# The norm's sum of squares as two fp32r products, with pools reordered, sums in place, and a weight load in pieces

## The chip, the cores and the metric

One core of one Trainium2 chip. The metric is the device time of one execution in microseconds. The engines: PE multiplies matrices into PSUM (eight banks of 128 x 512 fp32), DVE, ACT and POOL work on SBUF tiles (DVE and ACT on PSUM too), and SP issues all DMAs, in order.

## The reference, cut to what matters

Chunked attention over q, k, v (4 x 8 x 768 x 64) with 8 memory keys, then two feed-forward layers over 3072 tokens of 512 features:

```python
x = attention(q, k, v, mem_k, mem_v)            # 3072 x 512
h = x @ w_in                                    # 512 -> 2048
g = h * np.tanh(softplus(h))
x = g @ w_out                                   # 2048 -> 512
rms = np.sqrt(np.mean(x * x, axis=-1, keepdims=True) + 1e-06)
xn = x / rms * rms_g
g = xn @ w_gate                                 # 512 -> 1536
out = (g / (1 + np.exp(-g)) * (xn @ w_val)) @ w_out2   # 1536 -> 512
```

## The kernel before

**Numbers in two parts.** A factor is split by `split` (lines 144 to 146) into a high part, cast to fp32r by ACT, and a low part, the difference, by DVE (POOL for some weights). A product is then three matmuls: high by high, high by low, low by high. One product, of the norm, is left in plain fp32.

**Seven products for eight.** `group` (lines 616 to 642) computes a 2 x 2 block product from seven block products of sums, in the order 1, 6, 5, 4, 2, 7, 3, in four banks X, Y, Z, V; ACT and DVE take intermediate sums out of the banks, POOL adds one result. The weights' sums are made once by conversion jobs (`cv_all`; `finish`, line 268, for those w_in weights that were first kept unsummed), the activations' by `sum_pieces` (line 563): four subtractions and seven splits into tiles T.

**Stages.** (1) Attention, mixed with the first layer's first half for the token blocks that are ready: `unit` (plain products) for the first two blocks, then `group1` for the pairs. Results g go to a scratch in HBM. (2) `out1` (line 773): for each of six blocks m of 512 tokens, eight steps i; `Feed` loads g, applies Mish on ACT, splits it and PE multiplies it with w_out into four banks. A step is 24 matmuls. When a block is done, `rms_pieces` (line 784) makes the norm: squares on ACT, three additions on POOL, a product of ones with the sum, which adds over partitions (`p1`, line 800), then the root and the scaling on ACT and DVE. Its pieces are issued one by one between the next block's steps; every second block the T sums of a pair follow and are stored (`nt_scratch`). The last norm runs during the first groups of the next stage. (3) `group2`: twelve weights for each of three pairs; the result s goes to `h_scratch`. (4) `group3` (line 844): twelve units of 128 x 2 x 2 tokens against w_out2; the T tiles of a unit are made by `h_pieces` (line 841) between the seven products of the group before (`preparing`, line 1143). `h_load` (line 823) loads the unit's four blocks b11, b21, b12, b22, for odd units into weight slot 2. The last weight, ("o2", 5), is loaded into slot 3 (line 1176) when group2 of weight 10 no longer needs it.

**Memory.** `cp`, `gp`, `tp` hold group1's temporaries, its results g and the T tiles; they lie in this order on the left of SBUF and are closed after the last group1. The late pools take the same memory from its start: `gl` (4 KB a partition), `c` (2 x 2 KB) and `t` (8 x 8 KB). With `reuse_waits="tile"` a late tile waits for those earlier tiles that lay at its place. `gl` and `gr` hold one tile each for group2's v; `v_temp` (line 555) takes the same two for the temporaries of `sum_pieces`. `sm` (in `cvp`) is one tile of 4 KB.

**What sets the order.** The program is written as pieces issued between products (`between` functions with fixed slots). Then a planner (`schedule_with_timeline_sim`, line 19) orders each engine's instructions by a clock of its own: what is ready by that clock may go ahead of what stands before it. `pin` (`keep_in_program_order`) sets an instruction behind the one that stood before it in the program on its engine. On each engine, and on SP, the queue then runs in that order; an instruction that waits holds all behind it. A tile of a pool is given out in the planner's order too.

Of the kernel before, what the change touches and what calls it, by code (L numbers as in the profile page):

```python
# [29 lines left out]
def tile_kernel(  # L30
# [15 lines left out]
    nc = tc.nc  # L46
# [36 lines left out]
    rawp = ctx.enter_context(tc.tile_pool(name="rawp", bufs=2))  # L83
    cap = ctx.enter_context(tc.tile_pool(name="cap", bufs=3))
    mid_stack = ExitStack()
    cp = mid_stack.enter_context(tc.tile_pool(name="cp", bufs=6))
    gp = mid_stack.enter_context(tc.tile_pool(name="gp", bufs=5))
    tp = mid_stack.enter_context(tc.tile_pool(name="tp", bufs=8))
    late_pools = {}
    psp = ctx.enter_context(tc.tile_pool(name="psp", bufs=1, space=bass.MemoryType.PSUM))  # L90
    bk = [psp.tile([128, 512], F32, name=f"bk{c}") for c in range(6)]
# [3 lines left out]

    ident = const.tile([128, 128], F32, name="ident")
    ones = const.tile([128, 1], F32, name="ones")
    rmsg = const.tile([128, KC], F32, name="rmsg")


# [18 lines left out]
    def as7(s):  # L119
        return s.rearrange("p (a l f) -> p a l f", a=7, l=2)  # L120

    def w_load(key, u):
        s = w_slot(u)
        nc.sync.dma_start(out=s.bitcast(F32), in_=wd[key].bitcast(F32))
        wtab[key] = as7(s)

    def w_store(key, half):
# [140 lines left out]
    def finish(key):  # L268
        w = wtab[key]
        aa = [cap.tile([128, 512], F32, tag="ca", name="ca") for n in range(2)]  # L270
        for n, a in enumerate(aa):
            hi, lo = (w[:, 2 * n:2 * n + 2, l, :].bitcast(F32) for l in range(2))
            nc.vector.tensor_tensor(a.rearrange("p (a f) -> p a f", a=2), hi, lo, op=ALU.add)
        a0, a1 = aa
        a11, a12, a21, a22 = a0[:, 0:256], a0[:, 256:512], a1[:, 0:256], a1[:, 256:512]
        sm = cvp.tile([128, 4, 256], F32, tag="sm", name="sm")
        s4, s1, s2, s3 = (sm[:, i, :] for i in range(4))
        nc.gpsimd.tensor_tensor(s1, a21, a22, op=ALU.add)
        nc.gpsimd.tensor_tensor(s3, a11, a21, op=ALU.subtract)
# [278 lines left out]
    def t_pieces(j, x0, x1, new, temp_new, dram, tab):  # L558

        return sum_pieces(j, x0[:, 0:2, :], x0[:, 2:4, :], x1[:, 0:2, :], x1[:, 2:4, :],  # L560
                          new, temp_new, dram, tab)

    def sum_pieces(j, b11, b21, b12, b22, new, temp_new, dram, tab):
        cols = b11.shape[2]
        size = b11.shape[1] * cols
        temp = {}

        def as_block(x):
            return x[:, 0:size].rearrange("p (a n) -> p a n", n=cols)

        def one(p, src):
            t = new()
            if isinstance(t, tuple):
                split(src, *t)
                for l in range(2):
                    store_later(dram[:, p - 1, l].bitcast(F32), t[l].bitcast(F32))
                return
            v = t.rearrange("p l a n -> p l (a n)")[:, :, 0:size]
            v = v.rearrange("p l (a n) -> p l a n", n=cols)
            split(src, v[:, 0], v[:, 1])  # L580
            if dram is not None:
                store_later(dram[:, p - 1].bitcast(F32), t.bitcast(F32))
            tab[j, p] = v

        def sums():
            for p in (2, 4):
                temp[p] = as_block(temp_new(p).rearrange("p a n -> p (a n)"))
            nc.vector.tensor_tensor(b11, b12, b11, op=ALU.subtract)
            nc.vector.tensor_tensor(temp[2], b22, b11, op=ALU.subtract)
            nc.vector.tensor_tensor(temp[4], temp[2], b21, op=ALU.subtract)  # L590
            nc.vector.tensor_tensor(b12, b22, b12, op=ALU.subtract)

        early = [lambda: one(1, b11), sums]
        rest = [lambda: one(6, temp[2]), lambda: one(5, b11), lambda: one(4, temp[4]),
                lambda: one(2, b21), lambda: one(7, b12), lambda: one(3, b22)]
        return early, rest

# [18 lines left out]
    def group(mul, banks, n_, c12, c21, c22, temps):  # L616

        X, Y, Z, V = banks
        x, y, z, vv = (b_[:, 0:n_] for b_ in banks)
        s1, u2, z5 = temps()  # L620
        mul(1, X, True)
        nc.scalar.copy(s1, x)  # L622
        yield
        mul(6, Y, True)
        nc.vector.tensor_tensor(u2, y, s1, op=ALU.add)
        yield
        mul(5, Z, True)
        nc.scalar.copy(z5, z)
        yield
        mul(4, V, True)  # L630
        yield
        mul(2, X, False)
        yield
        mul(7, Y, False)
        u3 = s1
        nc.vector.tensor_tensor(u3, y, s1, op=ALU.add)  # L636
        yield
        mul(3, Z, False)
        nc.vector.tensor_tensor(c12, z, u2, op=ALU.add)
        nc.gpsimd.tensor_tensor(c22, u3, z5, op=ALU.add)  # L640
# [140 lines left out]

    xn = {}

    def rms_pieces(m, n, new, sq_new):
        xs = new().bitcast(F32).rearrange("p a b n -> p (a b) n")
        xn[n] = xs
        ps = banks1(m)
# [10 lines left out]
                nc.vector.tensor_copy(xs[:, c, :], ps[c])  # L798

        def p1():  # L800
            nc.tensor.matmul(ps[3], ones.to_broadcast([128, 128]), sq[0])
            nc.vector.tensor_scalar(mm, ps[3], 1.0 / DM, EPS_RMS, op0=ALU.mult, op1=ALU.add)

        def p2():
# [34 lines left out]
        hraw[n] = parts  # L839

    def h_pieces(n):
        return sum_pieces(n, *hraw.pop(n), t_new2, v_temp, None, ttab_h)

    def group3(n, j, r, between):
        o = s_new()
# [15 lines left out]
        run([group(mul, banks, 256, c12, c21, c22, lambda: (c_new()[:, 0:256], c12, c22))], between)  # L861
        nc.scalar.copy(o[0][:, 0:256], c11)
        for a in range(2):
            row = (2 * j + a) * N2 + 128 * r
# [5 lines left out]
    for x in vw:  # L870
        nc.gpsimd.memset(x, 0.0)
        nc.gpsimd.memset(x[:, :, :, D:D + 1], 1.0)
    nc.gpsimd.memset(ones, 1.0)

    CV_START = 24
    W_SLOT = (0, 4, 3, 2, 1, 0, 4, 3)
# [171 lines left out]
    late_pools["gl"] = late_pool("gl", 1)  # L1048
    late_pools["c"] = late_pool("c", 2)
    late_pools["t"] = late_pool("t", 8)  # L1050
    pend = []
    sq_new = lambda: [c_new() for _ in range(2)]
    for s, (m, i) in enumerate(steps):
        t = feed.next(s)
        out1(m, i, t)
        flush()
        if i == F1 // 2 - 1 and m < NB2 - 1:
            assert not pend
            p0, pend = rms_pieces(m, m, t_new2, sq_new)
            p0()  # L1060
            if m % 2:
                def both(m=m):
# [29 lines left out]
    def last_temp(p):  # L1092
# [5 lines left out]
    p0, pend = rms_pieces(  # L1098
        NB2 - 1, NB2 - 1,
        lambda: hold[:, 0:4 * N2].rearrange("p (a b n) -> p a b n", a=2, b=2),  # L1100
        lambda: [upper[:, a] for a in range(2)],
    )
    p0()

# [55 lines left out]
    for jn, j in enumerate(jback):  # L1160
# [7 lines left out]
        for f in range(HG + 2 if jn else HG, F2):  # L1168
            run([group2(j, f)], preparing(0, bt) if last and f == F2 - 1 else bt)
            if last and f == HG + 2:  # L1170
                w_load(("o2", 3), 5)
            elif last and f == HG + 3:
                h_load(0, *units[0])
                w_load(("o2", 4), 6)
            elif last and f == HG + 4:
                w_load(("o2", 5), 3)
    h_load(1, *units[1])
    for n, (j, r) in enumerate(units):
        if 0 < n < len(units) - 1:
# [34 lines left out]
```

## Time and profile before

| | us |
|---|---|
| median of 3 runs | 1191.08 (1189.69 to 1196.43) |
| the profiled execution | 1190.69 |
| its span in the trace | 1188.9 |
| PE busy | 1153.8 |
| DVE busy | 817.5 |
| ACT busy | 621.5 |
| POOL busy | 215.1 |

A row of the timeline has the start, the length, the engine, the line, the operation, output and inputs with their shapes, and in brackets how long the engine stood idle before it and what it waited for. Successive matmuls overlap: the distance of starts, not the length, is what one takes of PE's time. PEclk is the granted clock of TensorE as a share of 2.4 GHz; a value between 0.5 and 1 is a mean over the two levels.

### The profile page before, as it was taken

What the parts mean: (1) busy time and instruction counts of PE and PEld (TensorE: products, weight loads), DVE (VectorE), ACT (ScalarE), POOL (GpSimd) and SP (SyncE); (2) the same over time, 40 slices, a digit from 0 to 9 for tenths busy, and PEclk for the clock granted to TensorE, in tenths of its full rate; (3) what the DMA queues carried; (4) which work ended last, traced back from release to release, by engine and by line L of the source; (5) the groups of instructions that cost most, each with busy time, mean ns of one, the idle gap of its engine ahead of it and who ended that gap; (6) DMA issues with size and microseconds to landing.
All of it is one profiled execution on the core that took longest, in us unless ns stands there. A gap on an engine that the chain in (4) does not pass through costs nothing.

```text
span 1188.9 us, 22951 instructions
## 1 busy us (share of the span) xinstructions
PE 1153.8 (97%) x9052; PEld 1008.5 (85%) x9052; DVE 817.5 (69%) x1212; ACT 621.5 (52%) x996; POOL 215.1 (18%) x185
## 2 busy tenths in 40 slices
PE   6899899999999899999999999999999999999998
PEld 4789899999999688888878878878888888999998
DVE  4655898854755856675775675976886746887773
ACT  5566566543545866667665443553454423444442
POOL 2010222310132411030131121322221211000000
PEclk8899989999999999999999999999999999999999
DMA  9889869899488764595589388899889878654420
GB/s 188 172 230 217 209 239 264 231 293 300 148 304 289 246 204 129 187 362 163 195 329 393 144 343 333 321 416 391 319 312 377 315 264 293 195 173 142 142 90 36
DMA packets 219132, 294.20 MB, mean 247 GB/s; under 512 B 104208, under 2 KB 168720, under 8 KB 210064
## 3 DMA queue, kind: packets, MB, share of 16 engines
q1 hardware_dynamic: 219024, 292.73, 74.1%
q8 instruction: 71, 1.16, 0.4%
q14 instruction: 37, 0.30, 0.1%
HBM read 181.80 MB, written 110.89 MB: 246 GB/s over the span
## 4 chain that ended last, share of the span: by engine, by line
PE 74%; DMA 8%; DVE 7%; ACT 5%; issue 3%; POOL 2%; SPq 0%; ACTq 0%; POOLq 0%; DVEq 0%
PE bk L612 13%; PE bk L614 12%; PE bk L613 12%; DMA s<-g_scratch 4%; PE bk L856 4%; PE bk L854 4%; PE bk L855 4%; PE bk L726 3%; PE bk L727 3%; PE bk L725 3%; PE bkp L612 2%; PE bkp L614 2%; PE bkp L613 2%; PE bkp L434 2%; PE bkp L483 1%
## 5 line engine op out<-in xcount | busy, mean ns | idle before, releaser
L612 PE MATMUL bk<-T,w 128*128 128x384 f32 (+1 forms) x860 | 317.3, 372 | 5.5 <-ACT g L662 4.1
L613 PE MATMUL bk<-T,w 128*128 128x384 f32 (+1 forms) x860 | 312.5, 363 | 0.0
L614 PE MATMUL bk<-T,w 128*128 128x384 f32 (+1 forms) x860 | 311.6, 364 | 0.0
L612 PEld LDWEIGHTS bk<-T,w 128*128 128x128 f32 x860 | 162.7, 190 | 26.7 <-ACT g L662 4.3
L613 PEld LDWEIGHTS bk<-T,w 128*128 128x128 f32 x860 | 162.5, 189 | 17.3 <-issue 0.2
L614 PEld LDWEIGHTS bk<-T,w 128*128 128x128 f32 x860 | 162.3, 189 | 16.8
L854 PE MATMUL bk<-w,T 128*128 128x256 f32 x396 | 112.3, 284 | 2.9 <-ACT T L145 1.8
L725 PE MATMUL bk<-T,w 128*128 128x512 f32 x276 | 109.1, 396 | 2.9 <-ACT T L145 2.9
L856 PE MATMUL bk<-w,T 128*128 128x256 f32 x396 | 111.4, 282 | 0.2 <-DVE T L146 0.2
L855 PE MATMUL bk<-w,T 128*128 128x256 f32 x396 | 111.4, 281 | 0.0
L726 PE MATMUL bk<-T,w 128*128 128x512 f32 x276 | 109.4, 396 | 0.3 <-DVE T L146 0.3
L727 PE MATMUL bk<-T,w 128*128 128x512 f32 x276 | 108.6, 393 | 0.0
L640 POOL TENSOR_TENSOR v<-c,v 128x512 f32<-128x512 f32 x36 | 51.6, 1436 | 222.3 <-DVE c L636 164.8
L636 DVE TENSOR_TENSOR c<-bk,c 128x512 f32<-128x512 f32 (+2 forms) x72 | 43.1, 599 | 63.4 <-PE bk L614 51.7
L622 ACT COPY c<-bk 128x512 f32<-128x512 f32 (+2 forms) x72 | 37.0, 516 | 83.9 <-PE bk L614 33.3
L146 DVE TENSOR_TENSOR T<-s,T 128x1024 fp32r<-128x1024 f32 (+1 forms) x50 | 61.3, 1235 | 26.0 <-ACT T L145 25.5
L854 PEld LDWEIGHTS bk<-w,T 128*128 128x128 f32 x396 | 75.2, 190 | 4.2 <-ACT T L145 2.9
L855 PEld LDWEIGHTS bk<-w,T 128*128 128x128 f32 x396 | 75.5, 191 | 0.1
L856 PEld LDWEIGHTS bk<-w,T 128*128 128x128 f32 x396 | 75.0, 190 | 0.4 <-DVE T L146 0.4
L753 ACT ACTIVATE s<-s 128x1024 f32<-128x1024 f32 x44 | 46.7, 1061 | 38.6 <-DMA s<-g_scratch 36.6
L725 PEld LDWEIGHTS bk<-T,w 128*128 128x128 f32 x276 | 51.8, 188 | 15.4 <-ACT T L145 3.3
L726 PEld LDWEIGHTS bk<-T,w 128*128 128x128 f32 x276 | 52.0, 188 | 13.2 <-issue 1.2
(218 smaller groups left out, 2309.2 us busy)
## 6 DMA issues: line engine op xcount, KB each, us to landing
T<-nt_scratch SPq DMA_DIRECT2D x35, 1024.0 KB
g_scratch<-g SPq DMA_DIRECT2D x64, 384.0 KB
s<-g_scratch SPq DMA_DIRECT2D x46, 512.0 KB
h_scratch<-s SPq DMA_DIRECT2D x36, 512.0 KB
w<-wg SPq DMA_DIRECT2D x10, 1792.0 KB
wg<-w SPq DMA_DIRECT2D x30, 512.0 KB
raw<-in_moe_w_out_dram SPq DMA_DIRECT2D x28, 512.0 KB
nt_scratch<-T SPq DMA_DIRECT2D x14, 1024.0 KB
```

The costliest lines, as they stand in the source:

```text
L146: keep((eng or nc.vector).tensor_tensor(lo, src, hi.bitcast(F32), op=ALU.subtract))
L612: nc.tensor.matmul(ps, whi, xh, start=first and kk == 0, stop=False, **more)
L613: nc.tensor.matmul(ps, whi, xl, start=False, stop=False, **more)
L614: nc.tensor.matmul(ps, wlo, xh, start=False, stop=kk == 1, **more)
L640: nc.gpsimd.tensor_tensor(c22, u3, z5, op=ALU.add)
L725: nc.tensor.matmul(ps, ahi, bhi, start=start, stop=False)
L726: nc.tensor.matmul(ps, ahi, blo, start=False, stop=False)
L727: nc.tensor.matmul(ps, alo, bhi, start=False, stop=stop)
L753: nc.scalar.activation(x, g, self.act)
L854: nc.tensor.matmul(ps, t[:, 0, f], w[:, 0], start=first and f == 0, stop=False, **more)
L855: nc.tensor.matmul(ps, t[:, 0, f], w[:, 1], start=False, stop=False, **more)
L856: nc.tensor.matmul(ps, t[:, 1, f], w[:, 0], start=False, stop=f == HG - 1, **more)
```

## The change

Six edits. (a) The pools are opened in the order tp, gp, cp, and Feed's fourth split is called right after the late pools are opened. (b) `p1` splits the sum of squares into a high and a low part (tiles gl and gr in turn, for the last block the tile sm) and multiplies both with ones in fp32r, into the same bank; `ones_r` is a cast copy of ones. The norms advance the counter that alternates gl and gr in group2. (c) `finish` pins its two first additions for the w_in weights 6 and 5. (d) `h_pieces` no longer uses `sum_pieces`: the sums are made in place in b11 and b12, with no temporaries, in the order T1, 5, 6, 2, 4, 7, 3. (e) group3's product 5 comes before 6. (f) The load of ("o2", 5) is three DMAs: the factor of product 1 (256 KB), those of 2, 4 and 3, and those of 5, 6 and 7 (768 KB each). `sum_one` is the former inner function `one`, unchanged.

```diff
@@ pools
+    tp = mid_stack.enter_context(tc.tile_pool(name="tp", bufs=8))
+    gp = mid_stack.enter_context(tc.tile_pool(name="gp", bufs=5))
     cp = mid_stack.enter_context(tc.tile_pool(name="cp", bufs=6))
-    gp = mid_stack.enter_context(tc.tile_pool(name="gp", bufs=5))
-    tp = mid_stack.enter_context(tc.tile_pool(name="tp", bufs=8))
...
+    ones_r = const.tile([128, 1], F32R, name="ones_r")
...
-    def w_load(key, u):
+    def w_load(key, u, cuts=()):
         s = w_slot(u)
-        nc.sync.dma_start(out=s.bitcast(F32), in_=wd[key].bitcast(F32))
+        edges = (0,) + cuts + (7,)
+        for a, b in zip(edges, edges[1:]):
+            at = slice(512 * a, 512 * b)
+            nc.sync.dma_start(out=s[:, at].bitcast(F32), in_=wd[key][:, at].bitcast(F32))
...
@@ finish
-            nc.vector.tensor_tensor(a.rearrange("p (a f) -> p a f", a=2), hi, lo, op=ALU.add)
+            ins = nc.vector.tensor_tensor(a.rearrange("p (a f) -> p a f", a=2), hi, lo, op=ALU.add)
+            if key[1] in (6, 5):
+                pin(ins)
...
@@ group
-        mul(6, Y, True)
-        nc.vector.tensor_tensor(u2, y, s1, op=ALU.add)
-        yield
-        mul(5, Z, True)
-        nc.scalar.copy(z5, z)
-        yield
+        for p in (5, 6) if five_first else (6, 5):
+            if p == 6:
+                mul(6, Y, True)
+                nc.vector.tensor_tensor(u2, y, s1, op=ALU.add)
+            else:
+                mul(5, Z, True)
+                nc.scalar.copy(z5, z)
+            yield
...
@@ rms_pieces
         def p1():
-            nc.tensor.matmul(ps[3], ones.to_broadcast([128, 128]), sq[0])
+            parts = parts_new()
+            split(sq[0], parts[0], parts[1])
+            for l in range(2):
+                nc.tensor.matmul(
+                    ps[3], ones_r.to_broadcast([128, 128]), parts[l], start=l == 0, stop=l == 1
+                )
             nc.vector.tensor_scalar(mm, ps[3], 1.0 / DM, EPS_RMS, op0=ALU.mult, op1=ALU.add)
...
     def h_pieces(n):
-        return sum_pieces(n, *hraw.pop(n), t_new2, v_temp, None, ttab_h)
+        b11, b21, b12, b22 = hraw.pop(n)
+        one = lambda p, src: sum_one(n, p, src, t_new2, None, ttab_h)
+        sub = lambda out, a, b: nc.vector.tensor_tensor(out, a, b, op=ALU.subtract)
+        early = [lambda: one(1, b11), lambda: sub(b11, b12, b11), lambda: sub(b12, b22, b12)]
+
+        def p5():
+            one(5, b11)
+            sub(b11, b22, b11)
+
+        def p6():
+            one(6, b11)
+            sub(b11, b11, b21)
+
+        return early, [p5, p6, lambda: one(2, b21), lambda: one(4, b11),
+                       lambda: one(7, b12), lambda: one(3, b22)]
...
+    nc.scalar.copy(ones_r, ones)
...
     late_pools["t"] = late_pool("t", 8)
+    feed.split(4)
...
+    def v_parts():
+        n_v[0] += 1
+        x = v_new(n_v[0]).bitcast(F32R)
+        return [x[:, l, :] for l in range(2)]
...
-                w_load(("o2", 5), 3)
+                w_load(("o2", 5), 3, (1, 4))
```

## Rows read from the trace of the kernel before

**Rows 1.** The page, part 1: busy time, share of the span, instructions.

```profile
PE 1153.8 (97%) x9052; PEld 1008.5 (85%) x9052; DVE 817.5 (69%) x1212; ACT 621.5 (52%) x996; POOL 215.1 (18%) x185
```

**Rows 2.** Busy time by stretch: length, engines, PEclk, DMA share, GB/s.

```profile
145.00:150.00 5.00, 1.23 (x4) 1.23 (x5) 5.00 (x7) 2.49 (x5) 1.66 (x2) 0.81 1.07 310
...
150.00:155.00 5.00, 5.00 (x70) 4.02 (x68) 5.00 (x9) 5.00 (x10) 0.00 (x0) 0.51 0.89 353
...
396.00:400.00 4.00, 3.71 (x10) 2.61 (x10) 3.97 (x6) 4.00 (x6) 0.00 (x0) 0.66 0.21 59
...
1040.00:1160.00 120.00, 120.00 (x1008) 120.00 (x1007) 96.14 (x123) 53.73 (x81) 8.73 (x8) 1.00 0.45 137
```

**Rows 3.** Timeline of PE, 392 to 401 us: start, length.

```profile
392.53 0.40 PE L727 MATMUL bkp<-w 128*128 128x512 f32 x1
...
395.80 0.73 PE L725 MATMUL bk<-T,w 128*128 128x512 f32 x2 [2.87 <-ACT T L145]
...
400.81 0.40 PE L725 MATMUL bk<-T,w 128*128 128x512 f32 x1
```

**Rows 4.** Timeline of ACT, 387 to 396 us.

```profile
387.74 1.06 ACT L753 ACTIVATE sm<-w 128x1024 f32<-128x1024 f32 x1 [0.19 <-DVE w L146]
...
394.70 1.05 ACT L145 CAST T<-sm 128x1024 fp32r<-128x1024 f32 x1 [0.94 <-DMA g_scratch<-g]
```

**Rows 5.** Timeline of PE around the first product with ones.

```profile
436.27 0.40 PE L727 MATMUL bk<-T,w 128*128 128x512 f32 x1
...
437.59 0.39 PE L726 MATMUL bk<-T,w 128*128 128x512 f32 x1
...
437.82 0.40 PE L727 MATMUL bk<-T,w 128*128 128x512 f32 x1
```

**Rows 6.** Timeline of PE at the fifth norm, then groups by form.

```profile
616.85 1.12 PE L801 MATMUL bkp<-c,ones 128*128 128x512 f32 x2 [0.42 <-POOL c L796]
...
L753 ACT ACTIVATE s<-s 128x1024 f32<-128x1024 f32 x44 | 46.7, 1061 | 38.6 <-DMA s<-g_scratch 36.6 <-DVE T L146 1.8
L146 DVE TENSOR_TENSOR w<-ca,w 128x512 fp32r<-128x512 f32 x31 | 23.7, 764 | 9.7 <-ACT w L145 9.6
L145 ACT CAST w<-ca 128x512 fp32r<-128x512 f32 x47 | 29.1, 618 | 17.1 <-DVE ca L208 14.7 <-DMA wg<-w 2.2
```

**Rows 7.** Timeline of DVE, then of PE, 140 to 149 us.

```profile
140.00 0.69 DVE L273 TENSOR_TENSOR ca<-w 128x512 f32<-128x512 f32 x1
...
141.40 1.28 DVE L273 TENSOR_TENSOR ca<-w 128x512 f32<-128x512 f32 x2
...
144.46 0.94 DVE L588 TENSOR_TENSOR xb<-xb 128x768 f32<-128x768 f32 x1
...
145.99 1.49 DVE L589 TENSOR_TENSOR g<-xb 128x768 f32<-128x768 f32 x1
...
148.77 0.69 PE L612 MATMUL bk<-T,w 128*128 128x384 f32 x1 [4.07 <-ACT g L662]
```

**Rows 8.** 1000 to 1030 us: stretches as in rows 2, timelines, chain of waits.

```profile
1000.00:1005.00 5.00, 3.46 (x22) 2.73 (x21) 4.61 (x6) 3.85 (x6) 0.00 (x0) 1.00 0.70 291
1020.00:1025.00 5.00, 3.56 (x23) 2.95 (x24) 5.00 (x8) 4.29 (x6) 0.00 (x0) 1.00 0.29 108
1025.00:1030.00 5.00, 5.00 (x44) 5.00 (x43) 4.97 (x7) 0.78 (x3) 0.00 (x0) 1.00 0.28 83
...
1001.74 0.95 DVE L590 TENSOR_TENSOR v<-v,raw 128x768 f32<-128x768 f32 x1
...
1003.13 0.39 PE L854 MATMUL bk<-w,T 128*128 128x256 f32 x1 [0.97 <-DMA w<-wo]
...
1005.93 0.59 ACT L628 COPY v<-bk 128x512 f32<-128x512 f32 x1
...
996.13 6.96 DMA w<-wo
...
1010.77 4.23 DMA w<-h_scratch
```

More of the change, by code (lines that the diff above doesn't have):

```diff
@@ L561, in t_pieces, with sum_one @@
                           new, temp_new, dram, tab)
+    def sum_one(j, p, src, new, dram, tab):
+        cols = src.shape[2]
+        size = src.shape[1] * cols
+        t = new()
+        if isinstance(t, tuple):
+            split(src, *t)
+            for l in range(2):
+                store_later(dram[:, p - 1, l].bitcast(F32), t[l].bitcast(F32))
+            return
+        v = t.rearrange("p l a n -> p l (a n)")[:, :, 0:size]
+        v = v.rearrange("p l (a n) -> p l a n", n=cols)
+        split(src, v[:, 0], v[:, 1])
+        if dram is not None:
+            store_later(dram[:, p - 1].bitcast(F32), t.bitcast(F32))
+        tab[j, p] = v
     def sum_pieces(j, b11, b21, b12, b22, new, temp_new, dram, tab):
@@ L569, in as_block @@
             return x[:, 0:size].rearrange("p (a n) -> p a n", n=cols)
[L571 to L583, printed above, removed]
+        one = lambda p, src: sum_one(j, p, src, new, dram, tab)
         def sums():
@@ L614, in product, with group @@
             nc.tensor.matmul(ps, wlo, xh, start=False, stop=kk == 1, **more)
-    def group(mul, banks, n_, c12, c21, c22, temps):
+    def group(mul, banks, n_, c12, c21, c22, temps, five_first=False):
         X, Y, Z, V = banks
@@ L782, in tile_kernel, with rms_pieces @@
     xn = {}
-    def rms_pieces(m, n, new, sq_new):
+    def rms_pieces(m, n, new, sq_new, parts_new):
         xs = new().bitcast(F32).rearrange("p a b n -> p (a b) n")
@@ L800, in p1 @@
         def p1():
-            nc.tensor.matmul(ps[3], ones.to_broadcast([128, 128]), sq[0])
+            parts = parts_new()
+            split(sq[0], parts[0], parts[1])
+            for l in range(2):
+                nc.tensor.matmul(
+                    ps[3], ones_r.to_broadcast([128, 128]), parts[l], start=l == 0, stop=l == 1
+                )
             nc.vector.tensor_scalar(mm, ps[3], 1.0 / DM, EPS_RMS, op0=ALU.mult, op1=ALU.add)
@@ L860, in group3 @@
         c12, c21, c22 = o[1][:, 0:256], o[0][:, 256:512], o[1][:, 256:512]
-        run([group(mul, banks, 256, c12, c21, c22, lambda: (c_new()[:, 0:256], c12, c22))], between)
+        run([group(mul, banks, 256, c12, c21, c22, lambda: (c_new()[:, 0:256], c12, c22),
+                   True)], between)
         nc.scalar.copy(o[0][:, 0:256], c11)
@@ L1050, in tile_kernel, with sm_parts @@
     late_pools["t"] = late_pool("t", 8)
+    feed.split(4)
     pend = []
     sq_new = lambda: [c_new() for _ in range(2)]
+    def v_parts():
+        n_v[0] += 1
+        x = v_new(n_v[0]).bitcast(F32R)
+        return [x[:, l, :] for l in range(2)]
+    def sm_parts():
+        x = cvp.tile([128, 4, 256], F32, tag="sm", name="sm")
+        x = x.rearrange("p a f -> p (a f)").bitcast(F32R).rearrange("p (a n) -> p a n", a=2)
+        return [x[:, l, :] for l in range(2)]
     for s, (m, i) in enumerate(steps):
@@ L1058, in tile_kernel @@
             assert not pend
-            p0, pend = rms_pieces(m, m, t_new2, sq_new)
+            p0, pend = rms_pieces(m, m, t_new2, sq_new, v_parts)
             p0()
@@ L1100, in tile_kernel @@
         lambda: hold[:, 0:4 * N2].rearrange("p (a b n) -> p a b n", a=2, b=2),
-        lambda: [upper[:, a] for a in range(2)],
+        lambda: [upper[:, a] for a in range(2)], sm_parts,
     )
```

## The prediction

> **What bounds the kernel now.** I read the page first, then busy time by stage, then PE's waits and the stretches around them. PE is busy for 1153.8 of the 1188.9 us, DVE for 69% [rows 1]; in the long inner stretches PE has no gap at all (120.00 us of 120.00, DVE 96.14) [rows 2]. So the time is PE's queue of products plus the places where that queue stands still. A change pays if it takes PE work away or closes such a place, and anything it adds to ACT, DVE or the DMA queues is free as long as PE does not wait for it. Three places bear on this diff.
>
> *Leaving the first attention phases, near 145 us.* PE is busy 1.23 us of 5 there, and the granted clock is 0.81, then 0.51 in the five microseconds behind [rows 2].
>
> *From the last group1 to out1, near 393 us.* A matmul starts at 392.53, the next at 395.80, and the normal step is back only at 400.81 [rows 3].
>
> *From group2 to group3, 1000 to 1025 us.* Two stretches of 5 us hold 22 and 23 matmuls where the next one holds 44 [rows 8].
>
> **The sum is made against the profiled execution, 1190.69 us** (span 1188.9, 1.8 around it); the median of the runs is 1191.08, so 0.4 is added at the end. A measurement of this kernel can tell about 0.5%, 6 us, from no change.
>
> **Pool order and the early fourth split: -5.2.** Step 3 of Feed is the first whose output goes into the late T pool. Its Mish is done at 388.8, but the cast into T starts at 394.70, released by a store of g [rows 4]: the first late T tiles lie on the memory of cp and gp, and gp's tiles are read by the stores of the last group1. PE waits 2.87 us for that cast [rows 3]. After the change tp lies first, so those T tiles lie on tp tiles, which the last group1's own products free before PE gets to step 2; split(4) also comes earlier in the program. The cast needs 1.05 us and can follow the Mish at once, some 3 us before PE has finished step 2 at 392.8. What is late next are the T tiles on gp, the sixth onward: the store has landed at 394.7, and at 24 matmuls of 0.23 us (5.6 us) a step they are wanted only some 25 us on. Price: from 392.76 (one step behind the last matmul) to 400.81 is 8.05 us, and twelve matmuls ran in it, which take 12 x 0.233 = 2.80 at the step of rows 5. So 5.25 us, 2.9 of it the wait with its tail and 2.3 the slow steps afterwards: the granted clock from 396 to 400 is 0.66 [rows 2], most of it at the lower of its two levels (1.2 of 2.4 GHz), which it fell to after PE had stood idle. Bounds 0 and 5.25; I take 5.2, since the Mish is done 5.9 us before the cast.
>
> **Sum of squares as two products: -2.3.** The fp32 product with ones is two records of L801. They and one plain matmul lie between the matmul that starts at 436.27 and the one that starts at 437.59; the next starts 0.23 later [rows 5]. Of the 1.32 us two plain steps are 0.47, so the product costs PE 0.86. The two fp32r products cost two plain steps, 0.47. Saved 0.39, six times: 2.3. Added in front: a cast on ACT (0.62) and a subtraction on DVE (0.76) of the same size [rows 6], 1.4 us of latency behind POOL's third add, and as much load on engines that have room. The planner knows both and sets the product later in PE's queue; PE has out1's products to run meanwhile, and the bank that the product writes is asked for again only a block later. At one norm PE already waits 0.42 us for POOL today [rows 6], so the cover is not thick. Bounds: 2.3 saved to the loss of the slower rival. The tiles for the parts (gl, gr, once sm) are idle then or released long before; cost 0. The copy that makes ones_r is 128x1; it is bounded either side by the 0.62 of a 128x512 cast, taken 0.
>
> **finish pinned for weights 6 and 5: -1.9.** DVE's adds of finish for 6 and 5 run at 140.00 and 141.40 (two) [rows 7], ahead of the tail that PE is about to need. The tail's first subtraction starts at 144.46, the second at 145.99 (1.49 us beside POOL's part of finish, where the first takes 0.94); then comes the cast, then ACT's copy g<-bk, and only this frees the bank that PE has waited 4.07 us for, at 148.77 [rows 7]. The pin sets the adds behind what DVE had before them in the program, the tail's. DVE then does 0.69 + 1.28 us less ahead of the tail, all of it on the path if the tail's input is there that early, and POOL's part of finish moves out from beside the second subtraction, 0.5. That is at most 2.5; the input of the first subtraction comes by an ACT copy that gains less, so I take 1.9 for the copy g<-bk. Behind the adds wait only finish's own splits, wanted a group later. Bounds: 0 (another filler takes the hole) to 6.5 (all 4.07, and the 2.4 that five microseconds at clock 0.51 lose [rows 2]); I take no gain of clock, because half of the wait stays.
>
> **In-place sums, five first, last load in pieces: -4.4.** In the last group2 the two temporaries of h_pieces sit in the tiles gl and gr that group2's v also uses. The second, written at 1001.74, is in the tile that group2's own copy v<-bk wants; that copy runs only at 1005.93 [rows 8], so group2's last products are late, slot 2 is read to the end, and the load of unit 1 into slot 2 goes out at 1010.77, its first part landing 4.23 us later [rows 8]. That is the hole at 1020: 23 matmuls for 44, so 21 x 5 / 44 = 2.4 us. Without temporaries the copy waits for nothing of h_pieces, slot 2 is free several microseconds sooner, and T5 needs two blocks where T6 needed three and two subtractions. The hole at 1000 has a wait for the first temporary's T and one of 0.97 for weight 5, issued at 996.13 and landed 6.96 later [rows 8]. It is 1.5 us by PE's busy time (3.46 of 5) and 2.5 by 22 of 44 matmuls, taken 2.0 since some of the 22 are the longer ones. The first product now needs the first 256 KB alone. Bounded by the 384 KB part that took 4.23 us in company, it lands by 1000.4; PE stood for it until 1003.13. The steps are a chain now (cast, low part and subtraction, none over the 0.95 of a subtraction [rows 8], for T1, T5 and T6, then T4's two: at most 10.5 us), but a unit lasts 14.9 us (126 matmuls, 1008 in 120 us [rows 2]), and DVE's instruction count is the same. Product 2's T is made ahead of 4's; it is asked for last but two, so nothing waits. Two more DMA issues on SP are behind loads that are not urgent: 0. Bounds 0 to 4.9, taken 4.4.
>
> The whole transfer of weight 5 ran at 264 GB/s (1792 KB in 6.96 us [rows 8]), beside other loads, and no row shows it in pieces. The Trainium skill's page DMA: Bandwidth & Descriptors (section Bandwidth) has a rule against the pieces: batch transfers to 1 MiB or more; all three are smaller. By its fixed cost of some 2 us a transfer (section Anatomy of one DMA) an estimate is 4 us more for the three than for the whole, and the sum would be that of the second rival, 1180.
>
> Sum: 5.2 + 2.3 + 1.9 + 4.4 = 13.8; 1190.7 - 13.8 + 0.4 = **1177**.
>
> **Rivals.** *Holes move (0.20).* The planner orders every engine by its own clock, and one edit shifts all that follows. If the conversion jobs that fill ACT and DVE near 393 stay ahead of the cast, and group2's last products are again set behind group3's first, only the 2.3 and the 1.9 are left: 1187. For it: ACT runs the casts of conversions between Mish and T today. Against: today's wait names a store, not ACT.
>
> *Pieces late (0.12).* The second product, five, needs the third piece, with its last three matmuls, some 4 us after the first needs the first piece. One after another at the 4.23 us of 384 KB [rows 8], three pieces would be there at 1008.8 at the latest, at best with the whole at 1003.1; in between PE waits in the second product instead of the first. The 2.0 of the first hole stay and 1.1 come on top: 1180. For it: the queue is busy then. Against: the parts of one queue need not follow one another.
>
> *Better (0.08).* The hole at 145 closes with its clock: 1177 - 4.6, about 1172, or a little under.
>
> *Slower (0.08): PE at the norm before the low part.* If PE's queue keeps the ones product where it is now, the cast stands behind two Mish (1.06 each) on ACT, then 0.62 and 0.76: 3.5 us [rows 6]. The idling of 2.87 us at 393 already cost 2.3 of clock, so 5.8 a norm; four of six give 23 us: 1200. It decides from about three and a half norms, 20 us. Against: the planner places the product by these very inputs.
>
> **How the numbers follow.** Forecast 0.52, rivals as given. Faster by over 0.5% (under 1185): 0.52 + 0.12 + 0.08 and 0.06 of the first rival, where the hole at 393 closes in part: 0.78. Same: the rest of that rival, 0.14. Slower: 0.08. The range runs from 1170, the upper bounds of the four parts (5.3, 2.3, 6.5, 4.9: 1172) with 2 us for what the planner shifts elsewhere, to 1188, the first rival with 1 us over; it leaves out the slower rival and a share of the ends.
>
> **What would show it.** Right: no wait of PE for T near 393, and a full granted clock there; ones products as two plain steps; the load into slot 2 issued before 1005; PE with 43 or 44 matmuls in every 5 us of group3; the hole at 147 near 2 us. Wrong: a wait of PE for the low part at a norm, a new hole anywhere after 150 us, or PE's total busy time not smaller by about 2 us.

## The result and the profile after

The changed kernel takes 1176.23 us (median of 6 runs, 1172.87 to 1182.27) against 1190.67 us for the kernel before in the same job: ratio 0.9878, 95% interval 0.9844 to 0.9911. The forecast of 1177 with its range of 1170 to 1188 held. The profiled execution took 1174.5 us, its span is 1172.6, so the two traces are 16.3 us apart where the medians are 14.4 apart; the ledger below is of the traces.

Part 1 of the page, after, answers to [rows 1]:

```profile
PE 1142.5 (97%) x9052; PEld 1005.8 (86%) x9052; DVE 825.4 (70%) x1218; ACT 620.2 (53%) x1000; POOL 211.6 (18%) x185
```

PE has as many products as before, is busy 11.3 us less, and idles about 5 us less (1172.6 - 1142.5 = 30.1 for 1188.9 - 1153.8 = 35.1). The products with ones account for 2.3 of that busy time, by their steps (0.39 saved six times); the rest is plain products that take less time each, many of them at the full clock instead of the low one.

**Where it came from.** Both traces hold 9052 matmuls, so they can be laid over each other by counting: the time at which the changed kernel has started as many matmuls as the old one had by time t, minus t. The columns are the kernel after and runs of the next section; what matters is the step from one line to the next, since the first 60 us scatter by some microseconds from run to run (waits for the first loads of k). The line at 145 lies inside the old kernel's wait (144.70 to 148.77), so some 0.5 of what was won there stands in it already.

| t (before), us | after | u_pool | u_split4 | u_pin | u_ones | u_end | x_end | c_last |
|---|---|---|---|---|---|---|---|---|
| 145 | -0.4 | -1.9 | 0.6 | 0.4 | 3.8 | -1.0 | -1.8 | -1.3 |
| 160 | -4.5 | -5.5 | -1.7 | 0.5 | 0.1 | -4.7 | -5.8 | -3.6 |
| 392 | -3.9 | -4.2 | -1.1 | 0.4 | 0.9 | -3.4 | -4.9 | -2.6 |
| 400.8 | -9.3 | -6.9 | -2.5 | -5.0 | -4.5 | -8.8 | -10.3 | -8.0 |
| 675 | -15.0 | -12.5 | -8.1 | -10.6 | -5.4 | -14.4 | -15.1 | -13.3 |
| 770 | -14.7 | -12.2 | -7.9 | -10.3 | -7.1 | -14.2 | -14.8 | -15.3 |
| 800 | -11.8 | -7.7 | -3.4 | -8.4 | -7.5 | -9.6 | -10.0 | -15.3 |
| 1000 | -12.5 | -8.6 | -4.0 | -9.0 | -8.9 | -10.6 | -10.9 | -16.0 |
| 1025 | -17.6 | -13.7 | -9.2 | -14.2 | -13.8 | -15.4 | -12.1 | -21.2 |
| 1180 | -16.6 | -12.7 | -8.2 | -13.2 | -12.8 | -14.4 | -11.1 | -20.2 |

So the column "after" reads: -4.1 at 145 to 160, +0.6 by 392, -5.4 at 393, -5.7 over out1, +0.3 and +2.9 in group2 (770 to 800), -0.7 by 1000, -5.1 at 1000 to 1025, +1.0 in group3. The prediction had -1.9, -5.2, -2.3 and -4.4, and nothing for the 2.9.

Each place in rows. Busy time by stretch of the kernel after, with the columns of [rows 2]; the first two answer to the first two there, the others lie where the holes of [rows 8] would:

```profile
145.00:150.00 5.00, 3.94 (x36) 3.02 (x37) 4.90 (x7) 5.00 (x10) 0.24 (x1) 1.00 1.21 252
150.00:155.00 5.00, 5.00 (x70) 4.03 (x69) 5.00 (x9) 3.22 (x8) 1.15 (x2) 1.00 1.00 405
...
991.00:996.00 5.00, 5.00 (x44) 5.00 (x43) 3.23 (x5) 1.21 (x2) 1.30 (x1) 1.00 1.13 322
996.00:1001.00 5.00, 5.00 (x44) 5.00 (x44) 3.71 (x5) 1.21 (x2) 0.00 (x0) 1.00 1.19 312
1001.00:1006.00 5.00, 5.00 (x44) 5.00 (x43) 4.20 (x8) 2.51 (x4) 0.74 (x1) 1.00 0.11 41
1006.00:1011.00 5.00, 5.00 (x44) 5.00 (x43) 4.97 (x7) 2.86 (x6) 0.00 (x0) 1.00 0.49 163
```

36 matmuls for 4 in the first stretch, and the granted clock is 1.00 in both where it was 0.81 and 0.51. In group3 every 5 us hold 44 matmuls.

The timeline of PE after, at 145 us (answers to the last of [rows 7]), at 389 us ([rows 3]), at the first product with ones ([rows 5]) and in group2:

```profile
145.84 0.44 PE L622 MATMUL bk<-T,w 128*128 128x384 f32 x1 [0.94 <-ACT g L674]
...
388.75 0.39 PE L739 MATMUL bkp<-w 128*128 128x512 f32 x1
388.98 0.61 PE L737 MATMUL bk<-T,w 128*128 128x512 f32 x2
...
430.25 0.39 PE L738 MATMUL bk<-T,w 128*128 128x512 f32 x1
430.48 0.40 PE L816 MATMUL bkp<-v,ones_r 128*128 128x512 f32 x1
430.72 0.39 PE L739 MATMUL bk<-T,w 128*128 128x512 f32 x1
...
765.64 0.50 PE L622 MATMUL bkp<-T,w 128*128 128x512 f32 x1 [2.00 <-ACT v L640]
```

The wait for ACT's copy g is 0.94 instead of 4.07. At 389 the products out of T follow the others without a gap. A product with ones is one plain step, 0.24 to the next start. The last row is new: 2.00 us for ACT.

What ACT does ahead of these, its timeline after (the first two rows answer to [rows 4]):

```profile
384.05 1.06 ACT L765 ACTIVATE sm<-w 128x1024 f32<-128x1024 f32 x1 [0.20 <-DVE w L150]
...
386.28 1.04 ACT L149 CAST T<-sm 128x1024 fp32r<-128x1024 f32 x1
...
763.96 1.14 ACT L149 CAST w<-sm 128x512 fp32r<-128x512 f32 x2 [2.85 <-DVE sm L261]
765.01 0.58 ACT L640 COPY v<-bkp 128x512 f32<-128x512 f32 x1
```

The cast into T runs 2.2 us after its Mish instead of 7. In group2 two casts of a conversion stand in ACT's queue ahead of the copy that frees PE's bank, and they wait themselves for DVE.

The waits of PE after, from 400 to 1170 us (total, times, longest):

```profile
PE bkp L622 <- ACT v L640: 2.0, 1, 2.0
PE bkp L622 <- DVE v L653: 1.4, 2, 0.8
PE bk L622 <- DVE v L653: 1.4, 1, 1.4
PE bk L622 <- DVE c L648: 0.8, 1, 0.8
PE bk L622 <- DMA T<-nt_scratch: 0.4, 1, 0.4
```

All five are in group2; no product with ones waits, and POOL's 0.42 of [rows 6] is gone.

SP's issues after (start, length of the issuing, what):

```profile
982.17 1.27 SPq L128 DMA_DIRECT2D w<-wo  x3
...
988.83 4.48 SPq L852 DMA_DIRECT2D w<-h_scratch  x4
```

In [rows 8] the weight was issued at 996.13 and the load of blocks at 1010.77. Most of these 14.0 and 21.9 us are the lead that the whole queue of products has by then, 12.5 at 1000. Against the products, the weight goes out 3.9 us ahead of the first one of group3 (986.06 here) where it was 1.6 before (997.75).

### The profile page after: what moved, and what is told of

Its sections match the earlier page's. It is cut to its first block, busy times and chain, and to the rows that moved or that the text cites. A ratio compares the mean times of both kernels' runs of the same rounds, so it can differ in the third digit from the quotient of the medians.

```text
span 1172.6 us, 22972 instructions
## 1 busy us (share of the span) xinstructions
PE 1142.5 (97%) x9052; PEld 1005.8 (86%) x9052; DVE 825.4 (70%) x1218; ACT 620.2 (53%) x1000; POOL 211.6 (18%) x185
## 4 chain that ended last, share of the span: by engine, by line
PE 85%; DVE 6%; DMA 4%; ACT 2%; issue 2%; POOL 0%; SPq 0%; ACTq 0%; DVEq 0%; POOLq 0%
PE bk L622 12%; PE bk L623 12%; PE bk L624 12%; PE bk L738 6%; PE bk L739 6%; PE bk L737 6%; PE bk L887 4%; PE bk L885 4%; PE bk L886 4%; PE bkp L739 2%; PE bkp L738 2%; PE bkp L737 2%; PE bkp L622 2%; PE bkp L624 2%; PE bkp L623 2%; PE bkp L440 2%
## 5 line engine op out<-in xcount | busy, mean ns | idle before, releaser
L622 PEld LDWEIGHTS bk<-T,w 128*128 128x128 f32 x860 | 161.4, 188 | 25.4 <-DVE v L653 1.8
L623 PEld LDWEIGHTS bk<-T,w 128*128 128x128 f32 x860 | 161.6, 188 | 16.7 <-DVE T L150 0.5
L624 PEld LDWEIGHTS bk<-T,w 128*128 128x128 f32 x860 | 161.5, 188 | 15.7
L738 PE MATMUL bk<-T,w 128*128 128x512 f32 x276 | 107.4, 389 | 0.0
L739 PE MATMUL bk<-T,w 128*128 128x512 f32 x276 | 107.1, 389 | 0.0
L737 PE MATMUL bk<-T,w 128*128 128x512 f32 x276 | 107.0, 389 | 0.0
L237 POOL TENSOR_TENSOR sm<-ca 128x256 f32<-128x256 f32 x21 | 30.7, 1461 | 179.5 <-DVE ca L212 175.5
L739 PEld LDWEIGHTS bk<-T,w 128*128 128x128 f32 x276 | 51.8, 188 | 10.9
```

The costliest lines, as they stand in the source:

```text
L622: nc.tensor.matmul(ps, whi, xh, start=first and kk == 0, stop=False, **more)
L737: nc.tensor.matmul(ps, ahi, bhi, start=start, stop=False)
L738: nc.tensor.matmul(ps, ahi, blo, start=False, stop=False)
L739: nc.tensor.matmul(ps, alo, bhi, start=False, stop=stop)
```

## The experiments

Every kernel is the changed one with the edit shown, except where said. Times are medians; ratios are to the kernel before on the same chip.

**u_pool: the old pool order, the early fourth split kept.**

```diff
-    tp = ... ; gp = ... ; cp = ...
+    cp = ... ; gp = ... ; tp = ...
```

> The changed kernel with the pools in their old order (cp, gp, tp), everything else as changed. Theory: the gain of 5.4 us around 393 us comes from where the first late T tiles lie; with the old order PE waits again about 2.9 us for the cast into T, which names a store of g, and the granted clock falls below full behind it: some 5 us slower than the changed kernel, near 1181. Rival (the early fourth split is what closes the hole): no wait above 0.5 us near 393, within 1 us of the changed kernel.

Measured: 1179.24, ratio 0.9925 (0.99 to 0.995). The order of every engine's queue is that of the changed kernel. ACT's timeline and PE's waits from 370 to 400:

```profile
383.84 1.06 ACT L765 ACTIVATE sm<-w 128x1024 f32<-128x1024 f32 x1 [0.19 <-DVE w L150]
...
389.61 1.04 ACT L149 CAST T<-sm 128x1024 fp32r<-128x1024 f32 x1 [3.44 <-DMA g_scratch<-g]
```

```profile
PE bk L737 <- ACT T L149: 1.8, 1, 1.8
```

The cast waits for a store of g again, 3.44 us: the late T tiles lie on gp's tiles once more. Since the split stands earlier in ACT's queue, PE loses only part: the step at 393 is 2.7 instead of 5.4. The wait is 1.8 and not the 2.9 expected, and the granted clock stayed at 1.00 behind it, which was not expected either.

**u_split4: the new pool order, without the early fourth split.**

```diff
-    feed.split(4)
```

> The changed kernel without the early call of Feed's fourth split, the pools in the new order. With the old pool order and the early split, 2.4 us of the 5.4 at 393 us came back. Theory: the place of the first late T tiles is the whole of it as far as a store is waited for, and the split's place in the program gives the rest; without it the cast stands later in ACT's queue, PE waits 1 to 2.5 us near 389 and the time is 1 to 3 us more than the changed kernel's (1176), with no store named as the releaser. Rival (the new pool order alone closes the hole): no wait over 0.5 us there, the time the same.

Measured: 1180.43, ratio 0.9912 (0.988 to 0.9945). PE's waits, 370 to 400:

```profile
PE bk L737 <- ACT T L149: 1.9, 1, 1.9
```

Its busy time in the five microseconds behind that wait:

```profile
393.94:398.94 5.00, 5.00 (x14) 3.67 (x15) 4.97 (x6) 5.00 (x8) 0.34 (x1) 0.66 0.33 115
```

The step at 393 is 1.5. ACT then casts T<-sm at 392.85, behind conversions that the planner put first; no store holds it. So neither half does it alone: 2.7 with the split, 1.5 with the pools, 5.4 with both. Pools free the memory, the early call puts the cast ahead in the queue, and either one missing leaves a wait of nearly 2 us. That 2.7 is more than 1.5 says nothing of which half is worth more: the waits are alike (1.8 and 1.9), but here the clock fell to 0.66 behind it, and in u_pool it did not.

**u_pin: finish without the pins.**

```diff
-            if key[1] in (6, 5):
-                pin(ins)
```

> The changed kernel without the two pins in finish; everything else as changed. Theory: DVE's additions of finish for 6 and 5 run ahead of the tail's subtractions again, PE waits about 4 us near 147 for the copy g<-bk, the granted clock falls to its lower level for some 5 us: 4 to 5 us slower, near 1179, of which 1 to 2 may come back by 200 us. Rival (the order near 145 changed for another reason, the pools or the copy for ones_r): the wait stays near 0.9 us and the time is the same.

Measured: 1175.08, ratio 0.9893 (0.9866 to 0.9919); by time not to be told from the changed kernel. Its timeline of PE and busy time from 145:

```profile
149.69 0.69 PE L620 MATMUL bk<-T,w 128*128 128x384 f32 x1 [3.99 <-ACT g L672]
```

```profile
145.00:150.00 5.00, 1.01 (x8) 0.77 (x7) 5.00 (x6) 1.57 (x3) 2.15 (x3) 0.79 1.04 278
150.00:155.00 5.00, 5.00 (x62) 4.47 (x61) 5.00 (x10) 5.00 (x10) 0.00 (x0) 0.52 1.00 399
```

The whole hole is back with its clock, and nothing is gained from 145 to 160; so the pins are what the 4.1 there come from. Counted from 145 to the end, its trace gains 13.6 where the changed kernel's gains 16.3: 2.7 of the 4.1 are left, since it loses less in group2 (1.9 at 770 to 800 for 2.9). The 1179 expected did not come: against the scatter of the runs the 2.7 are too little to be seen in the medians.

**u_ones: the products with ones in plain fp32 again.**

```diff
-            parts = parts_new(); split(...); two products with ones_r
+            nc.tensor.matmul(ps[3], ones.to_broadcast([128, 128]), sq[0])
```

> The changed kernel with the norm's product with ones in fp32 again, from the unsplit sum; everything else as changed. Theory: six products cost 0.39 us more of PE each, 2.3 us in all, and PE's busy time rises by about that: near 1178.5. Rival (the fp32 products cost more than their own length, since 5.0 us came in between 400 and 665 us): the time rises by 4 to 5 us and the steps of the matmuls between the norms become 0.2325 us where they are 0.2275 now. Second rival (the added split costs somewhere what the products save): within 1 us.

Measured: 1173.44 (1171.67 to 1178.21), ratio 0.9882 (0.9848 to 0.9915): as fast as the changed kernel, so the theory (1178.5) fell and the second rival held. The trace is of the slowest of its four runs (1178.21). PE's waits, 400 to 1170:

```profile
PE bkp L813 <- POOL c L808: 1.0, 1, 1.0
PE bk L622 <- DVE c L648: 0.8, 1, 0.8
PE bk L738 <- DVE T L150: 0.7, 1, 0.7
PE bk L622 <- DMA T<-nt_scratch: 0.2, 1, 0.2
```

Over out1 it gains 0.9 where the changed kernel gains 5.7, as it should; but it has none of the waits for v, so from 675 to 800 it gains 2.0 where the changed kernel loses 3.1. The two products give 4.8 us (six times 0.39, the rest at the two waits of out1 in this list, for POOL's c and DVE's T, which the changed kernel has not) and take 5.1 back 150 us later, in a stage in which only the last norm has a part.

**u_end: the old end of the program** (sums with temporaries, product 6 before 5, weight 5 in one load), the norms still advancing the gl and gr counter; and **x_end**, the same with the norms on a counter of their own, so that group2's last v lies in the tile it had before.

```diff
 u_end: h_pieces, group3 and the last w_load as in the kernel before
 x_end: as u_end, and in v_parts
-        n_v[0] += 1
-        x = v_new(n_v[0]).bitcast(F32R)
+        n_p[0] += 1
+        x = v_new(n_p[0]).bitcast(F32R)
```

> The changed kernel with the end as before: h_pieces by sum_pieces with its two temporaries, product 6 before 5, the load of (o2, 5) in one piece. Theory: the two holes between group2 and group3 come back, 4 to 5 us, near 1179, with group2's copy v<-bk late behind a temporary's low part and the load into slot 2 issued as late against group2's end as before. Rival (the holes went because earlier edits shifted the order): no hole over 1 us there, the time the same.

> The end as in the kernel before (temporaries, 6 before 5, load in one piece), and the norms no longer advance the counter that alternates gl and gr, so the last group2's v lies in gr again as in the kernel before, where without this it lies in gl. All else as changed. Theory: with the old end alone the holes between 1000 and 1025 us stayed away because the second temporary no longer shares its tile with the last group2's v; with the counter as before they come back: 4 to 5 us slower than with the old end alone (near 1181), and the copy v<-bk of the last group2 behind the second temporary's cast. Rival (the planner's order around the last group2 differs for another reason): no hole, the time within 1 us of the old end alone (1176.9).

Measured: u_end 1176.89, ratio 0.9906 (0.9877 to 0.9935), with no wait of PE from 960 to 1030; x_end 1179.11, ratio 0.9909 (0.9877 to 0.9941). By time these two can't be told apart; their traces can. PE's waits of x_end, 960 to 1030:

```profile
PE bk L871 <- ACT T L149: 1.3, 2, 1.0
PE bk L871 <- DMA w<-wo: 1.1, 1, 1.1
```

And its busy time by stretch:

```profile
1005.00:1010.00 5.00, 3.97 (x30) 3.50 (x29) 5.00 (x8) 2.22 (x3) 1.33 (x1) 1.00 0.37 128
1010.00:1015.00 5.00, 4.60 (x36) 4.39 (x37) 5.00 (x6) 3.39 (x6) 0.00 (x0) 1.00 0.29 108
```

The last group2's copy v<-bk on ACT, in u_end and in x_end:

```profile
988.82 0.59 ACT L640 COPY v<-bk 128x512 f32<-128x512 f32 x1 [1.13 <-DVE v L600]
...
992.95 0.59 ACT L640 COPY v<-bk 128x512 f32<-128x512 f32 x1
```

The holes are back in x_end: 30 and 36 matmuls for 44. From 1000 to 1025 it gains 1.2, u_end 4.8. The only difference is which of gl and gr group2's v takes. In u_end the copy runs ahead of ACT's cast out of the second temporary (989.30), in x_end behind it (989.75) and three more, and group2's last six products then start at 997.09 instead of 992.06. So the cause of the hole is the shared tile, as the prediction said, and two things close it, each alone: sums in place (u_ones, which has the old counter and new sums, gains 4.9 there), or the counter that five of the six norms happen to shift (u_end, old sums).

**u_cuts: weight 5 in one load, all else changed.**

```diff
-                w_load(("o2", 5), 3, (1, 4))
+                w_load(("o2", 5), 3)
```

> The changed kernel with the load of (o2, 5) in one piece. Theory: PE reaches the first product of group3 several microseconds after the load went out at 982 us, with the whole transfer taking some 7 us, so PE waits for it by 0 to 1.5 us at the first product's last matmuls: 0 to 1.5 us slower. Rival (pieces cost by their number): the time 1 us or more shorter with one piece, since nothing waits for three.

Measured: 1174.9 in one run, 0.4 from the profiled execution of the changed kernel, with no wait of PE for the weight; from 1000 to 1025 it gains 5.1 like the changed kernel. The pieces are worth nothing here, either way: with all of group2's products ahead of group3's long run, the whole load goes out 3.9 us ahead of the first product of group3 (982.91 and 986.80), as the pieces do. Nor does the Trainium skill's rule of 1 MiB and more a transfer (page DMA: Bandwidth & Descriptors, section Bandwidth), weighed in the prediction, cost anything here (the page measures transfers issued by GpSimd, these are issued by SP); since nothing waits for that load, no run shows what the pieces themselves take.

**again: the kernel before, once more,** to see which waits belong to it.

> The kernel before once more, for a second trace of it. Of 5.0 us that came in between 400 and 665 us about 2.4 are the six products' length and 0.4 a wait; some 2 us are steps of 0.2325 us of the plain matmuls in places, against 0.2275 in the changed kernel. Theory: the slow steps belong to that execution and not to the kernel, so this trace shows them elsewhere or not at all (46 matmuls in ten microseconds of out1 between the norms). Rival (they belong to the kernel, such as to the fp32 products): the same places have 45 again. The waits at 147, 393, 1000 and 1020 us are to be the same within 0.5 us.

Measured: 1191.16. The waits at 147, 393, 1000 and 1020 are all there, and its ledger against the first trace stays within 1.1 us everywhere. Three are the same within 0.5 us (4.28, 1.08 and 1.04), but the one at 393 is not, 1.82 for 2.87:

```profile
395.11 0.73 PE L725 MATMUL bk<-T,w 128*128 128x512 f32 x2 [1.82 <-ACT T L145]
```

So the hole that the pool order closes is 1.3 us smaller in this trace. The slow steps stand at the same places as in the first one: the theory fell, they belong to the kernel.

**x_lat: the split of each norm's sum made twice,** which makes its parts about 1.4 us later.

```diff
             split(sq[0], parts[0], parts[1])
+            split(sq[0], parts[0], parts[1])
```

> The split of each norm's sum of squares is made twice, so that the high and the low part come some 1.4 us later and ACT and DVE have 1.4 us more a norm. The rival that gave 1200 (PE's queue keeps the product with ones where it was and stands until the low part is there) expects each of the first five norms to make PE wait 1 us or more and the time to rise by 7 us or more, to 1182 and over. My theory (the planner knows how long the split takes and sets the product later behind other products) expects no wait of PE at the products with ones over 0.5 us, and a time within 3 us of the changed kernel: 1173 to 1178.

Measured: 1178.16 in one run, 3.7 above the changed kernel's profiled execution: between the theories. Its timeline of PE at the third norm:

```profile
516.61 0.49 PE L817 MATMUL bkp<-v,ones_r 128*128 128x512 f32 x1
...
527.80 1.20 PE L737 MATMUL bk<-T,w 128*128 128x512 f32 x4 [1.36 <-ACT T L149]
530.48 0.79 PE L738 MATMUL bk<-T,w 128*128 128x512 f32 x1 [1.48 <-DVE T L150]
```

```profile
530.00:535.00 5.00, 4.52 (x14) 3.64 (x15) 3.90 (x5) 1.37 (x3) 0.96 (x2) 0.66 0.67 199
```

No product with ones waits, as I held. But behind the third norm, Mish, casts and the norm's scaling are late on ACT and DVE, PE waits twice for T, and the clock falls to 0.66: 4.8 us are lost there by the ledger. The work that the split adds is what can hurt, not the place of the product; once a norm there was room for it, twice there was not at one norm of six. Part of it may be the planner's order: it set two Mish (524.81) ahead of both casts into T (526.72), where in the changed kernel a cast follows each Mish. The run doesn't separate the two.

**c_last, c_ct, c_v: only the last norm changed,** since its parts use the tile sm, which the conversions in group2 use too.

```diff
 c_last: the last norm in plain fp32, the five others as two products
 c_ct:   the last norm's parts in two tiles of the pool c
 c_v:    the last norm's parts in gl or gr
```

> The last norm alone goes back to the plain fp32 product with ones, so its parts no longer take the one tile sm, which the weight conversions of group2 use as well; the five norms before it keep the two products. Theory 'tile': because the last norm's parts pass through sm, the conversions that need sm are set later, and their two casts come to stand ahead of the copy v<-bkp that PE waits 2.00 us for at 765.64; without sm in the norm the waits between 765 and 800 go. Expected: no wait of PE over 1 us for ACT's copies there, the trace 2 to 3 us ahead of the changed kernel by 800, minus 0.4 for the one fp32 product: 1171 to 1173 for its 1174.5 to 1176. Rival 'planner': any split in a norm moves the planner's order, waits of 2 to 3 us in all stay somewhere in group2: 1174 to 1177.

> The last norm keeps its two products, but its parts go into two tiles of the pool c instead of sm. Theory 'tile': the waits between 765 and 800 go as in the run with the last norm in fp32, and the 0.4 of the product is kept: 1171 to 1173. Rival 'planner': the order shifts again and waits of 2 to 3 us in all stay in group2: 1174 to 1177. A third way: the pool c has two tiles only, which group2 uses for its temporaries; then PE waits for them near the first groups, at 680 to 710, and up to 3 us are lost there: 1175 to 1179.

> The last norm's parts go into one of the tiles gl and gr that group2's v uses, as those of the other norms do. Theory 'tile': the conversions get sm earlier and the waits between 765 and 800 go; since the last norm runs beside the first groups of group2, whose v is in the same two tiles, up to 2 us may be lost near 680 to 700 instead: 1171 to 1176. It also shifts the alternation of gl and gr by one, so that the hole at 1000 to 1025 could come back, at 3.2 us between the two kernels that differ in it: then 1175 to 1179. Rival 'planner': waits of 2 to 3 us stay between 765 and 800.

Measured: c_last 1170.33 (1169.4 to 1171.0), ratio 0.9835 (0.9817 to 0.9852); c_ct 1182.57, ratio 0.9939 (0.9922 to 0.9956); c_v 1177.04, ratio 0.989 (0.9872 to 0.9908). PE's waits from 400 to 1170, c_last:

```profile
PE bk L622 <- DVE c L648: 0.8, 1, 0.8
PE bk L622 <- DMA T<-nt_scratch: 0.4, 1, 0.4
```

c_ct (first three of five):

```profile
PE bk L622 <- DMA T<-nt_scratch: 4.3, 4, 2.3
PE bkp L622 <- DMA T<-nt_scratch: 2.4, 1, 2.4
PE bk L622 <- ACT s L730: 2.2, 2, 1.2
```

c_v, its one wait, and the clock in the five microseconds behind it:

```profile
PE bkp L622 <- DVE v L653: 7.0, 1, 7.0
```

```profile
668.88:673.88 5.00, 5.00 (x13) 3.95 (x14) 4.59 (x5) 2.72 (x5) 0.89 (x1) 0.54 0.63 252
```

In all three the 2.00 us for ACT's copy v are gone, so they do hang on the last norm's split with its parts in sm. In c_last the copy stands ahead of the two casts (760.32, the first of them 761.43) that it stands behind in the changed kernel. But what comes instead is different each time: nothing, 6.7 us of waits for loads of T, 7.0 for one addition on DVE that stands behind the last norm's scaling and four subtractions. So c_ct and c_v missed what theory 'tile' expected of them (1171 to 1173, 1171 to 1176), and only c_last's time came near it. c_last is the best version by its median, 3.5 us below the changed kernel in the profiled executions and 5.9 in the medians; by ratio the two intervals still touch (0.9852 and 0.9844). The theory in its plain form falls, though: the last norm has done with sm at 647.9 (its second product with ones starts at 647.5), and the conversions write sm only from 731.68 on, as POOL's timeline of the changed kernel shows:

```profile
731.68 1.05 POOL L237 TENSOR_TENSOR sm<-ca 128x256 f32<-128x256 f32 x1 [0.69 <-DVE ca L212]
```

No conversion waits for that tile. What the split changes is the planner's order of what follows; by which step of its clock was not tried.

## Why the prediction was right, and where not

**The total** was right to 1 us, of terms that missed by up to 3.4 and a loss that no term had: 13.8 predicted, 16.3 between the traces, 14.4 between the medians. That the sum came so close is partly luck.

*Pool order and the early split, -5.2:* measured -5.4, and by the mechanism given: a store of g holds the cast (u_pool), it is gone, and the clock stays full. What the step left open, that the earlier call is needed as much as the pools, u_split4 shows. The trace before had it: a conversion's cast that waits itself stands ahead until 393.8, and the store holds the cast into T only 0.94 longer.

```profile
393.14 0.62 ACT L145 CAST w<-ca 128x512 fp32r<-128x512 f32 x1 [2.42 <-DVE ca L208]
```

*Sum of squares, -2.3:* the product itself is right: one plain step each, no wait at any norm, 0.39 saved six times. The term was mis-sized at -2.3: out1 gained 5.7. The wait for POOL at the fifth norm is gone, which is worth 0.7 (the stretch that takes 1.32 us at the first norm takes 2.01 there). The other 2.5 or so are plain steps that are slightly longer in stretches of the old kernel: ten of them from 439.69 take 2.10 us to the tenth start there, and 2.04 from 439.80 in the new one, 111 for 112 matmuls in 25 us. They stand in both traces of the old kernel, but not in u_ones, whose ones products are fp32 too, nor in any other run that takes an edit back. What slows them stays open. And by time the two products paid nothing: u_ones without them is as fast, for the reason under *What no term had*.

*The pins, -1.9:* mis-sized; -4.1 in the trace of the changed kernel, and nothing without the pins (u_pin). The step said that half of the wait stays and so took no gain of clock. In this trace a wait of 0.94 stayed, not 2.2, and behind it the clock held at 1.00: the slow steps went with the wait. This is the case that stood as the rival *better*; some 0.6 came back by 392. But the size is partly luck. Eleven traces here have the pins and the same queues up to 385 us, and the wait at 145 is 0.94 to 2.04 in them (0.94 in two, 1.54 or more in nine). In seven the clock stays full behind it, and 145 to 160 gains 3.6 to 4.1; in four (u_split4, u_cuts, c_last, c_v) it is 0.66 or 0.67 for five microseconds, and the gain is 2.1 to 2.4. So the half of the wait that the step left is what most executions show, and the gain of clock that it took at nothing comes in some and not in others.

*The end, -4.4:* measured -5.1. The step about the shared tile is right (x_end), but two of its parts do nothing: the load in pieces (u_cuts), and the in-place sums as soon as the counter is shifted (u_end). The counter stood in the diff, and the prediction took it to cost nothing without asking what it may bring.

*What no term had:* the 2.9 us in group2 (4.5 to 4.9 in u_pool, u_end and x_end, whose queues are the same there, but whose clock fell behind the wait). A new hole after 150 us stood among the prediction's signs of being wrong, and it came. The first rival said that one edit shifts all that follows, but looked for that only at the holes it knew. c_last, which keeps five of the six split norms, shows that it was avoidable: taken over 675 to 800, it gains 2.0 where the changed kernel loses 3.1.

*The rivals:* holes moved neither at 393 nor at 1000. Pieces late: no wait for the weight. PE at the norm before the low part: not even with twice the split (x_lat). In the end 1177 was reached by the pins paying 2.2 more, the norm 3.4 more and the end 0.7 more than their terms, and group2 and the drift between the stages giving most of it back; no term of the sum foresaw that balance.

## What to carry to other kernels

Where a planner orders the queues, cost an edit at its own place from the rows, but allow some microseconds in stages it does not touch, and then lay the two traces over each other by the count of matmuls: a gain given back 150 us later is seen at once, while the totals hide it. If such a loss shows, undo the edit at one of its places instead of everywhere (here one norm of six). And the slow steps behind a wait can go with it or stay, with the same queues, so price a shortened wait as a range, with them and without, and don't take one trace for the size.

## What the runs showed that I had not expected

**The length of a stop alone does not say what the clock does.** u_pool runs the queues of the changed kernel, and PE waits 2.0 us for the same copy v in both. The five microseconds behind that wait, the changed kernel first, then u_pool:

```profile
765.64:770.64 5.00, 5.00 (x22) 4.15 (x23) 2.08 (x4) 2.26 (x4) 0.00 (x0) 1.00 1.02 399
768.10:773.10 5.00, 5.00 (x15) 3.95 (x16) 2.08 (x4) 1.92 (x4) 0.00 (x0) 0.66 1.03 402
```

The granted clock also stayed at 1.00 behind 0.94 (after, 145.84), 1.8 (u_pool, 390.71), 2.23 (u_cuts, 766.35) and 2.40 us (c_ct, 654.58). It was 0.66 behind 1.08 (again, 1002.74), 1.93 (u_split4, 393.94) and 2.87 [rows 2, 3], 0.52 behind 3.99 (u_pin), 0.54 behind 7.0 (c_v), and 0.66 behind two waits of 1.36 and 1.48 within 3 us (x_lat). So between 1 and 2.4 us these traces have both, and what decides is not shown. Of a mean like 0.52 most is at the lower of the two levels.

**Two products for one fp32 product are less work for PE.** The fp32 product with ones took 0.86 us [rows 5], the two fp32r ones 0.24 each.

**The start scatters.** At equal count of matmuls the kernels here lie between -2.1 and +4.1 us of the old one by 60 us, in code that mostly is the same; differences below that size between two single traces have to be read from their steps, not from their ends.
